# Low parts of the probabilities split in two halves, and tiny two-tensor operations issued as plain tensor products, in an attention and two-layer MLP kernel ordered by a planner

## The chip, the cores and the metric

The kernel runs on one core of one Trainium2 chip. The time is device microseconds (us) of one execution; the kernel before took 744.99 us in the median of three runs (744.27 to 745.95). The engines are called PE (matrix multiply), ACT (activations), DVE (vector), POOL (GpSimd) and SP (which issues the DMAs here).

## The reference

Attention with a hashed mask over 2 batches, 8 heads, 768 positions and a head size of 64, and then two MLPs over the 1536 tokens of width 512 with a hidden width of 2048:

```python
q_bits = (einsum('bhsd,dk->bhsk', q, proj) > 0); k_bits likewise     # 6 hash bits
mask   = q_bucket[..., :, None] == k_bucket[..., None, :]
scores = where(mask, q @ k.T / 8, -1e9);  scores -= max(scores)
attn   = exp(scores);  attn /= sum(attn) + 1e-9;  o = attn @ v
x = o as (tokens, 512)
x = silu(x @ moe_w_in) @ moe_w_out
x = hardswish(x @ moe2_w_in) @ moe2_w_out          # h * clip(h + 3, 0, 6) / 6
```

q, k, v and proj are float32, the weights float64. The kernel multiplies in float16 pairs: a value is split into a high part and a low part (what the high part lost), and a product is three matmuls: high by high, low by high, high by low.

## The kernel before, in words

**Attention.** A pair is two heads of one batch (8 pairs, 4 a batch). A unit is one pair and two of its six query tiles of 128 rows, so it has four slots (two tiles by two heads); there are 24 units and 96 slots. For each slot PE makes the 768 scores in PSUM (L819, L820); DVE takes their maximum (L823) and two tiny products of it (L825 `sc`, L828 `nb`); ACT takes the exponential and its sum (L831 into `e`, float32). The score buffers `s` are two, so the scores of a slot wait for the exponential of the slot two before it. Then there are two ways. In the first 32 slots (`exact_values`, two of three blocks of batch 0) PE turns `e` in float32 (L847), ACT copies the turned tile (L853; the planner may give a copy to DVE, L854) and PE multiplies by the values (L859). In the other 64 (`split_values`) ACT casts `e` to float16, the high part (L878; DVE instead is L879), POOL takes the low part `e - high` into the second half of the tile `PN` (L880), one transposing DMA turns both (L883), and PE multiplies (L873). At the end of a unit (`finish`) DVE makes reciprocals of the sums (L900, L903 and, for exact units, L905) and scales (L908), ACT and POOL split the result (L912, L913), a DMA turns it, and ACT squares it for a norm (L425).

**Weights and MLPs.** Each weight chunk of 512 KB arrives by DMA in a buffer `st` (three of them), with 64-bit words that ACT (L489), POOL (L490) and DVE (L492, L494) put together; then ACT (L431) and DVE (L437) split it into high and low. In `mlp1` a hidden tile is made by PE (L946), passes ACT's tanh (L989), a DVE product (L991) and a split (ACT L431, DVE L437 into `G`), and PE multiplies it by the second weight (L1003). `mlp2` does the same with a relu (L1078 to L1086) and L1091. The MLP of batch 0 runs beside the attention of batch 1.

**Small scales.** Norms and scales are columns of one tile `table`, 128x1 each. `mul` (L419) multiplies two of them and a constant in one `scalar_tensor_tensor` (L420).

**What sets the order.** `Plan` holds every operation with its engine (or two engines to choose from), a cost, and what it reads and writes. `Plan.issue` lays out the work 24 times with lists of ranks, judges each by ten randomised replays, and issues the best in that order; each engine then runs its own list in order. A cost table (`Cost`) has waits between engines, a slack behind DMAs, and a shared port: POOL operations, and DVE operations whose entry ends in `True`, are laid out so that they don't overlap. So any change of a cost, of a flag or of the number of operations gives another order on all engines.

Of the kernel before, what the change touches and what calls it, by code (L numbers as in the profile page):

```python
# [247 lines left out]
class Plan:  # L248
# [6 lines left out]
    def op(self, ways, reads=(), writes=(), take=None, give=None, before=(), turn=0):  # L255

        o = Op(ways if isinstance(ways, list) else [ways], take, give, turn, len(self.ops))
        for cell in writes:  # L260
            o.deps.update(self.writers.get(cell, ()))
            o.deps.update(self.readers.get(cell, ()))
        for cell in reads:
            assert cell in self.writers, cell
            o.deps.update(self.writers[cell])
        for cell in (*reads, *writes):
            if isinstance(cell, tuple) and isinstance(cell[0], Buf):
                b = cell[0]
                assert not b.closed, (b.tag, cell[1:])
                if b.prev is not None:  # L270
                    o.deps.update(b.prev.ops)
                b.ops.append(o)
        for cell in writes:
            self.writers[cell], self.readers[cell] = [o], []
        for cell in reads:
            if cell not in writes:
                self.readers.setdefault(cell, []).append(o)
        for d in o.deps:
            d.succ.append(o)
        for d in before:  # L280
            d.soft.append(o)
        self.ops.append(o)
        return o
# [26 lines left out]
def kernel(  # L310
# [63 lines left out]
    def buf(pool, tag, shape, dtype, bufs=1):  # L374
        return Buf(plan, pool, tag, shape, dtype, bufs)
# [12 lines left out]
    ident = const("ident", [P, P])  # L388
    op((POOL, 0.3, lambda: make_identity(nc, ident)), (), ["ident"])
    op((DVE, 0.1, lambda: nc.vector.memset(three, 3.0)), (), ["three"])  # L390
    ident16 = buf(ep, "PN", [P, P], F16, bufs=3)
    op((DVE, 0.14, lambda: nc.vector.tensor_copy(ident16.t, ident)), ["ident"], [(ident16, 0)])

# [20 lines left out]
    def pow2(o, hx, sign, base):  # L414
        nc.vector.tensor_scalar(
            o.bitcast(I32), hx, float(sign * 2**23), float(base * 2**23), op0=ALU.mult, op1=ALU.add
        )

    def mul(o, a, b, c=1.0):  # L419
        nc.vector.scalar_tensor_tensor(o, a, c, b, op0=ALU.mult, op1=ALU.mult)  # L420

    def square_sum(src, dst, n, reads, writes):
        def fn():
# [175 lines left out]
    xparts = const("xparts", [P, B, NU, HP])  # L599
    vparts = const("vparts", [P, B, HP])  # L600
    v_s = [const(f"v_s{b}", [P, 1]) for b in range(B)]
    v_i = [const(f"v_i{b}", [P, 1]) for b in range(B)]
    XT = [None] * B

    def heads(x, b, h0, n):
# [2 lines left out]
    def v_norm(b):  # L608
        ss = small().tile([P, 1], F32, tag=f"vss{b}", name="vss")
        op((DVE, 0.15, lambda: nc.vector.tensor_reduce(ss, vparts[:, b], op=ALU.add, axis=AX.X)),  # L610
           [("vp", b, i) for i in range(HP)], [("vss", b)])
        key, tot = total(lambda: ss, 1, [("vss", b)])

        def fn():
            hx = half_exp(tot, 1)
            pow2(v_s[b], hx, -1, 203)
            pow2(v_i[b], hx, 1, 51)

        op((DVE, 0.35, fn), [key], [("v_s", b)], give="m")

# [172 lines left out]
    class Unit:  # L793
# [71 lines left out]
        def split_values(self, e, po, a, cell):  # L865
            V = self.pair.V
            pn = buf(ep, "PN", [P, 2, S], F16, bufs=NPN)
            pt = buf(ep, "PT", [P, 2, T, P], F16, bufs=NPT)

            def values():  # L870
                for kt in range(T):
                    for i, (vh, pl) in enumerate(combos):
                        nc.tensor.matmul(  # L873
                            po(), pt.t[:, pl, kt, :], V.t[:, a, vh, kt * D : (kt + 1) * D],
                            start=(i == 0 and kt == 0), stop=(i == 2 and kt == T - 1),
                        )

            op(ways((ACT, Cost.act(S), lambda: nc.scalar.activation(pn.t[:, 0], e.t, AF.Copy)),  # L878
                    (DVE, 0.47, lambda: nc.vector.tensor_copy(pn.t[:, 0], e.t), True)), [(e, 0)], [(pn, 0)])  # L879
            op(ways((POOL, Cost.pool_tt(S), lambda: nc.gpsimd.tensor_tensor(pn.t[:, 1], e.t, pn.t[:, 0], op=ALU.subtract)),  # L880
                    (DVE, Cost.tt(S), lambda: nc.vector.tensor_tensor(pn.t[:, 1], e.t, pn.t[:, 0], op=ALU.subtract), True)),
               [(e, 0), (pn, 0)], [(pn, 1)])
            op((SP, Cost.turn(2 * T), lambda: nc.sync.dma_start_transpose(  # L883
                out=pt.t.rearrange("p h t c -> p (h t) c"), in_=pn.t.rearrange("p h c -> p (h c)"))),
               [(pn, 0), (pn, 1)], [(pt, 0)], turn=1)
            op((PE, 3 * T * Cost.mm(D), values), [(pt, 0), (V, 0), (V, 1)], [cell])

        def finish(self):
            pr, n, nt = self.pair, self.n, self.nt
            cells = [(qi, a) for qi in range(nt) for a in range(2)]  # L890
            rc = buf(small, "rc", [P, 2 * QT], F32, bufs=4)
            x = buf(ep, "x", [P, 2 * QT, D], F32, bufs=2)
            xn = buf(ep, "xn", [P, QT, 2, P], F16)
            if XT[pr.b] is None:
                XT[pr.b] = buf(tp, ("X0", "T3")[pr.b], [P, NK, T, 2, P], F16)
            xt = XT[pr.b]
            xq = lambda: x.t[:, :n].rearrange("p (q a) d -> p q (a d)", a=2)

            def reciprocals():
                nc.vector.tensor_scalar(  # L900
                    rc.t[:, :n], self.sm.t[:, :nt].rearrange("p q a -> p (q a)"), 1e-9 * PSC, None, op0=ALU.add
                )
                nc.vector.reciprocal(rc.t[:, :n], rc.t[:, :n])  # L903
                if self.exact:
                    nc.vector.tensor_scalar(rc.t[:, :n], rc.t[:, :n], v_s[pr.b], None, op0=ALU.mult)  # L905

            op((DVE, 0.5 if self.exact else 0.3, reciprocals, True), [(self.sm, *c) for c in cells] + [("v_s", pr.b)], [(rc, 0)])
# [46 lines left out]
    def mlp1(b, blk, pool):  # L954
# [15 lines left out]

        op((DVE, 0.34, start), [tk], [("mlp", key)], give="m")
        for g in range(W1I.n):
            op((DVE, 0.14, lambda g=g: mul(u1[:, g : g + 1], v_i[b], W1I.i[:, g : g + 1], 0.5), True),
               [("v_s", b), ("W1I", g)], [("u1", key, g)])
        G = buf(pool, "G", [P, NF, 2, n], F16)

# [44 lines left out]
        def finish():  # L1021
            hx = half_exp(tot2, 1)
            pow2(c2, hx, -1, 203)
            pow2(ci, hx, 1, 51)
            mul(ci, ci, cgi)
            mul(ci, ci, v_i[b], 0.5)
            mul(ci, ci, W1I.top)
            mul(ci, ci, W1O.i)

        op((DVE, 1.05, finish, True), [tk, ("mlp", key), ("W1O", 0), ("W1I", "top"), ("v_s", b)], [("c2", key)], give="m")  # L1030
        for j in tiles:
            c2i[b, j] = ci, ("c2", key)
        for m in range(NK):
# [162 lines left out]
```

## Time and profile before

| what | value |
|---|---|
| median of three runs | 744.99 us |
| the profiled execution, whole | 746.96 us |
| its span, first to last instruction | 745.2 us |
| PE, ACT, DVE, POOL busy | 693.0, 519.1, 507.5, 184.3 us |
| mean granted PE clock | 0.986 of full speed |

The profile is of one execution, 1.97 us above the median; 1.76 us of it lie outside the span. Busy time is the union of an engine's instructions. A PE instruction that waits shows as idle time before it, with the engine whose signal came last. The stages can be told apart by what runs: up to 128.6 us (the first L946) attention of batch 0 with the first weights arriving; to 204.5 us (the last split of the first MLP's weights) that MLP starts while its weights are still split; to 361.9 us (the last L913) batch 1's attention beside the MLP of batch 0; then MLPs alone.

### The profile page before, as it was taken

The numbers are of one execution on the slowest core, as the hardware profiler recorded it, in microseconds if no ns is written. First come the engines' busy times: TensorE is split into PE (matmuls) and PEld (weight loads), VectorE is DVE, ScalarE is ACT, GpSimd is POOL, SyncE is SP. The second block draws the span as 40 slices with busy tenths as digits, with TensorE's granted clock in tenths as the row PEclk, the third lists the DMA queues.
The fourth block names the chain that finished last, engine by engine and source line by source line (L and its number), as shares of the span: only waits on it lengthen the run. The fifth ranks groups of instructions, "written<-read, shape, count | busy, mean of one in ns | idle before, by whom it ended". The sixth has DMA issues, their size and how long they took to land.

```text
span 745.2 us, 15604 instructions
## 1 busy us (share of the span) xinstructions
PE 693.0 (93%) x6060; PEld 514.1 (69%) x6060; DVE 507.5 (68%) x1147; ACT 519.1 (70%) x1027; POOL 184.3 (25%) x182
## 2 busy tenths in 40 slices
PE   3799988776899999999999999999999999999997
PEld 3498877654688888888888888864445664444564
DVE  4898999999976886986695968883333443333443
ACT  7998999899988988898665858872334334233433
POOL 3111224544364656667222220000000000000000
PEclk9999999997999999999999999999999999999999
DMA  8798556999599889989845450000000000000100
GB/s 303 184 244 191 159 187 219 209 237 251 117 172 209 162 198 199 205 156 162 208 144 178 159 174 1 1 1 1 1 0 35 23 1 29 0 1 1 57 1 28
DMA packets 176265, 89.61 MB, mean 120 GB/s; under 512 B 158784, under 2 KB 165952, under 8 KB 176192
## 3 DMA queue, kind: packets, MB, share of 16 engines
q1 hardware_dynamic: 176192, 88.63, 49.4%
q8 instruction: 47, 0.77, 0.4%
q14 instruction: 26, 0.21, 0.1%
HBM read 44.57 MB, written 3.15 MB: 64 GB/s over the span
## 4 chain that ended last, share of the span: by engine, by line
PE 73%; DVE 11%; ACT 9%; issue 3%; DMA 2%; POOL 1%; SPq 0%; ACTq 0%; DVEq 0%; POOLq 0%
PE h L946 27%; PE s L1091 17%; PE h L1003 16%; PE o L859 3%; PE o L873 3%; PE s L819 3%; PE s L820 3%; DVE nm L823 2%; ACT sq L425 2%; ACT e L831 2%; PE h L847 1%; DVE w L494 1%; DVE table L420 1%; ACT w L431 1%; DMA w<-in_v_dram 1%
## 5 line engine op out<-in xcount | busy, mean ns | idle before, releaser
L1091 PE MATMUL s<-y,G 128*128 128x512 f16 x576 | 134.4, 379 | 0.8 <-ACT w L1107 0.8
L1003 PE MATMUL h<-G,w 128*128 128x256 f16 x1152 | 133.6, 273 | 0.1
L946 PEld LDWEIGHTS <-w 128*128 128x128 f16 x1152 | 113.1, 100 | 27.7 <-DVE g L991 10.3
L880 POOL TENSOR_TENSOR PN<-e,PN 128x768 f16<-128x768 f32 x64 | 110.0, 1722 | 78.0 <-ACT PN L878 49.5
L1003 PEld LDWEIGHTS <-w 128*128 128x128 f16 x1152 | 110.9, 98 | 15.0 <-DVE w L437 0.4
L1078 ACT ACTIVATE g<-h,table 128x256 f32<-128x256 f32 x96 | 50.7, 562 | 88.7 <-PE h L946 88.7
L823 DVE TENSOR_REDUCE nm<-s 128x1 f32<-128x768 f32 x96 | 91.2, 951 | 21.1 <-PE s L820 20.5
L831 ACT ACTIVATE e<-s,nb,sc 128x768 f32<-128x768 f32 x96 | 95.6, 996 | 10.5 <-DVE nb L828 8.7
L1091 PEld LDWEIGHTS <-G 128*128 128x128 f16 x576 | 56.3, 98 | 62.8 <-issue 1.1
L1082 DVE TENSOR_SCALAR g<-g 128x512 f32<-128x512 f32 (+1 forms) x64 | 23.1, 360 | 101.7 <-ACT g L1078 101.7
L946 PEld LDWEIGHTS <-T 128*128 128x128 f16 x576 | 56.4, 98 | 42.1
L946 PE MATMUL h<-X,w 128*128 128x256 f16 x576 | 75.8, 282 | 9.7 <-DVE g L991 9.7
L490 POOL TENSOR_SCALAR st<-st 128x512 f32<-128x512 f32 x64 | 47.8, 749 | 149.2 <-ACT w L489 65.3
L1085 ACT ACTIVATE G<-g 128x512 f16<-128x512 f32 (+1 forms) x64 | 33.4, 522 | 62.0 <-DVE g L1084 62.0
L819 PE MATMUL s<-T 128*128 128x384 f16 x192 | 65.0, 339 | 9.2 <-ACT e L831 9.1
L820 PE MATMUL s<-T 128*128 128x384 f16 x192 | 65.2, 340 | 0.0
L946 PE MATMUL h<-T,w 128*128 128x256 f16 x576 | 64.3, 272 | 0.4 <-DVE g L991 0.4
L1086 DVE TENSOR_TENSOR G<-g,G 128x512 f16<-128x512 f32 (+1 forms) x64 | 35.7, 559 | 40.4 <-ACT G L1085 40.4
L878 ACT ACTIVATE PN<-e 128x768 f16<-128x768 f32 x63 | 52.9, 841 | 2.7 <-DMA PT<-PN 2.6
L946 PE MATMUL h<-T,T 128*128 128x512 f16 (+1 forms) x288 | 50.7, 326 | 0.0
L946 PE MATMUL h<-X,T 128*128 128x512 f16 (+1 forms) x288 | 50.7, 326 | 0.0
L859 PE MATMUL o<-w,PT 128*128 128x64 f32 x384 | 46.8, 272 | 2.2 <-DVE sc L825 2.2
(128 smaller groups left out, 1117.4 us busy)
## 6 DMA issues: line engine op xcount, KB each, us to landing
st<-in_moe_w_in_dram SPq DMA_DIRECT2D x32, 512.0 KB, 4.6
st<-in_moe_w_out_dram SPq DMA_DIRECT2D x32, 512.0 KB, 3.9
qk<-in_v_dram SPq DMA_DIRECT2D x8, 384.0 KB, 3.5
out_dram<-w SPq DMA_DIRECT2D x12, 256.0 KB, 2.0
qk<-in_q_dram SPq DMA_DIRECT2D x6, 384.0 KB, 3.4
qk<-in_k_dram SPq DMA_DIRECT2D x6, 384.0 KB, 5.4
w<-in_v_dram SPq DMA_DIRECT2D x2, 768.0 KB, 8.8
T<-T SPq DMA_DIRECT2D x8, 192.0 KB, 2.8
```

Of the source, the lines that this page charges most:

```text
L490: op((POOL, Cost.pool_ts(512), lambda: nc.gpsimd.tensor_scalar(st.t[:, :, 1].bitcast(F32), st.t[:, :, 1].bitcast(F32), 0.0, 1.0, op0=ALU.m ...
L819: nc.tensor.matmul(o, t.t[:, 0, c, :], t.t[:, 1, ks, :], start=True, stop=False)
L820: nc.tensor.matmul(o, t.t[:, 2, c, :], t.t[:, 3, ks, :], start=False, stop=True)
L823: op((DVE, 0.865, lambda: nc.vector.tensor_reduce(nm.t, ps.t[:, :, :HS], op=ALU.max, axis=AX.XY, negate=True)), [(ps, 0)], [(nm, 0)])
L831: op((ACT, 0.97, lambda: nc.scalar.activation(e.t.rearrange("p (n c) -> p n c", n=2), ps.t[:, :, :HS], AF.Exp, bias=nb.t, scale=sc.t, accu ...
L859: nc.tensor.matmul(po(), pt.t[:, kt, :], vraw.t[:, v0 + a, kt * D : (kt + 1) * D], start=(kt == 0), stop=(kt == T - 1))
L878: op(ways((ACT, Cost.act(S), lambda: nc.scalar.activation(pn.t[:, 0], e.t, AF.Copy)), (DVE, 0.47, lambda: nc.vector.tensor_copy(pn.t[:, 0] ...
L880: op(ways((POOL, Cost.pool_tt(S), lambda: nc.gpsimd.tensor_tensor(pn.t[:, 1], e.t, pn.t[:, 0], op=ALU.subtract)), (DVE, Cost.tt(S), lambda ...
L946: nc.tensor.matmul(ph, W[f, wl, kt, :], XT[b].t[:, kt, ts, xl, :], start=(c == 0), stop=(c == 3 * NK - 1))
L1003: nc.tensor.matmul(pf.t[:, :n], W1O[f, wl, slice(m * P, (m + 1) * P)], G.t[:, f, gl], start=(f == 0 and c == 0), stop=(f == NF - 1 and c = ...
L1078: nc.scalar.activation(g.t[:, cs], pf.t[:, cs], AF.Relu, bias=three, scale=a)
L1091: nc.tensor.matmul(acc[m // 2].t[:, m % 2, :DM], gs.t[:, f % 3, gl, m * P : (m + 1) * P], W2O[f, wl], start=(f == 0 and c == 0), stop=(f = ...
```

## The change

A third column `least` holds the constant that is added to the sums. `mul` without a constant is a `tensor_tensor` of two 128x1 columns, and the scale of V's inverse, `v_i`, is kept halved (`v_h`), so that two of its uses need no constant. The addition of `least` and the product by `v_s` in the reciprocals become `tensor_tensor` with a broadcast column. Three entries lose the flag of the shared port (the reciprocals, `u1`, and the end of `mlp1`). The low part of a probability tile is two operations of 384 columns instead of one of 768, each free to go to POOL or to DVE; the transposing DMA waits for both.

```diff
     def mul(o, a, b, c=1.0):
-        nc.vector.scalar_tensor_tensor(o, a, c, b, op0=ALU.mult, op1=ALU.mult)
+        if c == 1.0:
+            nc.vector.tensor_tensor(o, a, b, op=ALU.mult)
+        else:
+            nc.vector.scalar_tensor_tensor(o, a, c, b, op0=ALU.mult, op1=ALU.mult)
...
-            pow2(v_i[b], hx, 1, 51)
+            pow2(v_h[b], hx, 1, 50)
...
-            op(ways((POOL, Cost.pool_tt(S), lambda: nc.gpsimd.tensor_tensor(pn.t[:, 1], e.t, pn.t[:, 0], op=ALU.subtract)),
-                    (DVE, Cost.tt(S), lambda: nc.vector.tensor_tensor(pn.t[:, 1], e.t, pn.t[:, 0], op=ALU.subtract), True)),
-               [(e, 0), (pn, 0)], [(pn, 1)])
+            for n in range(2):
+                c = slice(n * HS, (n + 1) * HS)
+                op(ways((POOL, Cost.pool_tt(HS), lambda c=c: nc.gpsimd.tensor_tensor(
+                            pn.t[:, 1, c], e.t[:, c], pn.t[:, 0, c], op=ALU.subtract)),
+                        (DVE, Cost.tt(HS), lambda c=c: nc.vector.tensor_tensor(
+                            pn.t[:, 1, c], e.t[:, c], pn.t[:, 0, c], op=ALU.subtract), True)),
+                   [(e, 0), (pn, 0)], [(pn, 1 + n)])
...
-                nc.vector.tensor_scalar(
-                    rc.t[:, :n], self.sm.t[:, :nt].rearrange("p q a -> p (q a)"), 1e-9 * PSC, None, op0=ALU.add
+                nc.vector.tensor_tensor(
+                    rc.t[:, :n], self.sm.t[:, :nt].rearrange("p q a -> p (q a)"), least.to_broadcast([P, n]), op=ALU.add
                 )
                 nc.vector.reciprocal(rc.t[:, :n], rc.t[:, :n])
                 if self.exact:
-                    nc.vector.tensor_scalar(rc.t[:, :n], rc.t[:, :n], v_s[pr.b], None, op0=ALU.mult)
-            op((DVE, 0.5 if self.exact else 0.3, reciprocals, True), ...
+                    nc.vector.tensor_tensor(rc.t[:, :n], rc.t[:, :n], v_s[pr.b].to_broadcast([P, n]), op=ALU.mult)
+            op((DVE, 0.5 if self.exact else 0.3, reciprocals), ...
...
-        op((DVE, 1.05, finish, True), [tk, ("mlp", key), ("W1O", 0), ("W1I", "top"), ("v_s", b)], [("c2", key)], give="m")
+        op((DVE, 1.05, finish), [tk, ("mlp", key), ("W1O", 0), ("W1I", "top"), ("v_s", b)], [("c2", key)], give="m")
```

The counts of what is issued stay almost the same. The new program issues 54 of the 60 products of `table` columns as `tensor_tensor`; all 64 low parts are on POOL in both, as 128 halves now; one copy L853 that was DVE's (L854) is ACT's, one cast L878 goes from ACT to DVE, one tiny `sc` from DVE to POOL, and one split of `mlp1` (L1035) from POOL to ACT. Line numbers of the new program are higher (L880 is L889, L831 is L837, L991 is L1002, L437 is L442, L492 and L494 are L497 and L499).

On POOL, in the attention of batch 1, the rows before (`PN` is the tile of both parts, `e` the exponentials, `xn` the result of a unit):

```order
L880 TENSOR_TENSOR PN_3470<-e_3365,PN_3470 128x768
L880 TENSOR_TENSOR PN_3499<-e_3443,PN_3499 128x768
L880 TENSOR_TENSOR PN_3572<-e_3533,PN_3572 128x768
L913 TENSOR_TENSOR xn<-x_3234,xn 128x2x128
L880 TENSOR_TENSOR PN_3648<-e_3581,PN_3648 128x768
```

and now:

```order
L889 TENSOR_TENSOR PN_3648<-e_3605,PN_3648 128x384 x2
L889 TENSOR_TENSOR PN_3695<-e_3657,PN_3695 128x384 x2
L889 TENSOR_TENSOR PN_3751<-e_3706,PN_3751 128x384 x2
L924 TENSOR_TENSOR xn<-x_3266,xn 128x2x128
L889 TENSOR_TENSOR PN_3837<-e_3797,PN_3837 128x384 x2
```

Both halves of a tile stand together on POOL; none has gone to DVE.

On ACT, the rows that end with the 48th exponential of the program, before (`w` are weights being split, `sq` are squares):

```order
L831 ACTIVATE e_2808,sm_2774<-s_2627,nb_2713,sc_2700 128x768
L431 ACTIVATE w_2803<-w_1847,table 128x512 x3
L431 ACTIVATE G<-g_2794,table 128x2x256
L878 ACTIVATE PN_2864<-e_2808 128x768
L912 ACTIVATE xn<-x_2255 128x2x128
L431 ACTIVATE w_2882<-w_2237,table 128x512 x2
L831 ACTIVATE e_2902,sm_2774<-s_2779,nb_2885,sc_2835 128x768
L431 ACTIVATE w_2882<-w_2237,table 128x512 x2
L878 ACTIVATE PN_2932<-e_2902 128x768
L831 ACTIVATE e_2941,sm_2774<-s_2830,nb_2906,sc_2904 128x768
```

and now:

```order
L837 ACTIVATE e_2875,sm_2852<-s_2740,nb_2799,sc_2785 128x768
L923 ACTIVATE xn<-x_2424 128x2x128
L436 ACTIVATE w_2781<-w_1931,table 128x512
L884 ACTIVATE PN_2912<-e_2875 128x768
L837 ACTIVATE e_2923,sm_2852<-s_2858,nb_2910,sc_2907 128x768
L430 ACTIVATE sq,xparts<-x_2424 128x256
L884 ACTIVATE PN_2960<-e_2923 128x768
L430 ACTIVATE sq,xparts<-x_2790 128x256
L837 ACTIVATE e_2980,sm_2852<-s_2917,nb_2975,sc_2965 128x768
```

The splits of weights stand earlier than before, but counted from the start of the program the same work is ahead of this exponential: 288 instructions before and 290 now (accumulator reads not counted), the two more being a copy L853 and a square L425 of a unit's result. PE's list ahead of the scores two slots later differs by six L1003 more, all other counts being equal.

On DVE, from the last weight chunks of the second MLP to the 42nd hidden tile of `mlp1` (L991, the last block of batch 1), before (`y` and `T` are weight tiles, `st` arriving chunks):

```order
L494 SCALAR_TENSOR_TENSOR y_7206<-st_7216,y_7206 128x512
L492 SCALAR_TENSOR_TENSOR y_7206<-y_7206,st_7246 128x512
L1017 TENSOR_REDUCE table<-table 128x1
L494 SCALAR_TENSOR_TENSOR y_7206<-st_7246,y_7206 128x512
L508 TENSOR_REDUCE table<-table 128x1
L991 SCALAR_TENSOR_TENSOR g_7358<-g_7358,h_7311 128x512
L409 TENSOR_SCALAR hx<-p_tot 128x1
L415 TENSOR_SCALAR table<-hx 128x1 x2
L437 SCALAR_TENSOR_TENSOR G<-g_7358,table,G 128x2x256
L991 SCALAR_TENSOR_TENSOR g_7389<-g_7389,h_7343 128x512
```

and now:

```order
L442 SCALAR_TENSOR_TENSOR T_7356<-T_6468,table,T_7356 128x512
L1028 TENSOR_REDUCE table<-table 128x1
L499 SCALAR_TENSOR_TENSOR y_7305<-st_7287,y_7305 128x512
L497 SCALAR_TENSOR_TENSOR y_7305<-y_7305,st_7328 128x512
L442 SCALAR_TENSOR_TENSOR T_7356<-T_6468,table,T_7356 128x512
L499 SCALAR_TENSOR_TENSOR y_7305<-st_7328,y_7305 128x512
L1002 SCALAR_TENSOR_TENSOR g_7451<-g_7451,h_7401 128x512
L497 SCALAR_TENSOR_TENSOR y_7305<-y_7305,st_7367 128x512
L442 SCALAR_TENSOR_TENSOR T_7460<-y_6618,table,T_7460 128x512
L499 SCALAR_TENSOR_TENSOR y_7305<-st_7367,y_7305 128x512
L1002 SCALAR_TENSOR_TENSOR g_7483<-g_7483,h_7436 128x512
```

Thirteen splits of the second MLP's weights that stood behind this tile stand ahead of it now, between the rows that put the last chunks together, and the last chunk comes behind the 41st hidden tile; PE's list has the same rows ahead of this tile's matmuls but for one tiny sum.

## Rows read from the trace of the kernel before

**Rows 1.** The page, busy us (share) and instructions of each engine

```profile
PE 693.0 (93%) x6060; PEld 514.1 (69%) x6060; DVE 507.5 (68%) x1147; ACT 519.1 (70%) x1027; POOL 184.3 (25%) x182
```

**Rows 2.** Busy us by stretch, granted clock, DMA share, GB/s

```profile
0.00:20.00 20.00, 6.99 (x66) 6.25 (x67) 9.93 (x35) 15.36 (x28) 6.78 (x23) 1.00 0.85 294
20.00:207.00 187.00, 155.11 (x1451) 130.49 (x1451) 176.50 (x419) 180.69 (x363) 59.11 (x59) 0.95 0.80 199
207.00:460.00 253.00, 250.32 (x2922) 218.09 (x2919) 194.58 (x433) 203.08 (x409) 118.40 (x100) 1.00 0.77 171
460.00:745.20 285.20, 280.58 (x1631) 159.27 (x1628) 126.54 (x264) 120.00 (x230) 0.00 (x0) 1.00 0.03 12
```

**Rows 3.** What PE waited for, 120 to 205 us: total, times, longest

```profile
PE h L946 <- DVE g L991: 9.7, 4, 4.4
PE s L819 <- ACT e L831: 5.4, 5, 2.3
```

**Rows 4.** What ACT waited for, 20 to 200 us

```profile
ACT N L431 <- DVE qksc L415: 1.5, 1, 1.5
ACT e L831 <- DVE nb L828: 1.4, 3, 0.8
ACT G L431 <- DVE g L991: 1.1, 1, 1.1
```

**Rows 5.** The chain that ended last, 124 to 160 us: start, us, what

```profile
129.26 1.49 DVE table L420
...
136.90 1.86 DVE w L494
...
141.24 1.49 DVE table L420
...
148.56 2.05 DVE G L437
...
156.82 2.05 DVE w L494
```

**Rows 6.** Instructions of single lines: duration ns min/median/max, first and last start

```profile
L420 DVE SCALAR_TENSOR_TENSOR table<-table x60: 146/159/1490, 66.2 to 498.0; 128x1 f32<-128x1 f32 x60
L420 DVE SCALAR_TENSOR_TENSOR table<-inv x8: 159/160/1600, 7.6 to 252.8; 128x1 f32<-128x1 f32 x8
...
L437 DVE SCALAR_TENSOR_TENSOR G<-g,table,G x48: 721/746/2130, 148.5 to 473.3; 128x512 f16<-128x512 f32 x48
...
L494 DVE SCALAR_TENSOR_TENSOR w<-st,w x32: 675/682/2129, 17.3 to 175.6; 128x512 int32<-128x512 int32 x32
...
L900 DVE TENSOR_SCALAR rc<-sm x24: 154/160/635, 39.6 to 350.6; 128x4 f32<-128x4 f32 x24
...
L908 DVE TENSOR_TENSOR x<-o,rc x24: 406/415/426, 44.5 to 360.9; 128x256 f32<-128x256 f32 x24
```

**Rows 7.** Instructions on the tiles PN and xn, POOL's

```profile
L880 POOL TENSOR_TENSOR PN<-e,PN x64: 1639/1647/2376, 126.8 to 351.7; 128x768 f16<-128x768 f32 x64
...
L913 POOL TENSOR_TENSOR xn<-x,xn x24: 666/673/1403, 53.0 to 361.9; 128x256 f16<-128x256 f32 x24
```

**Rows 8.** Groups of instructions: busy us, mean ns, idle before

```profile
L1003 PE MATMUL h<-G,w 128*128 128x256 f16 x1152 | 133.6, 273 | 0.1
...
L853 ACT ACTIVATE PT<-h 128x384 f32<-128x384 f32 x63 | 28.7, 505 | 0.8 <-PE h L847 0.6
...
L425 ACT ACTIVATE sq<-x 128x256 bf16<-128x256 f32 x24 | 10.1, 422 | 0.9 <-DVE x L908 0.9
...
L437 DVE SCALAR_TENSOR_TENSOR T<-T,table,T 128x512 f16<-128x512 f32 x8 | 5.7, 744 | 0.0
...
L425 ACT ACTIVATION_READ_ACCUMULATOR sq<-x 128x1 f32 x24 | 5.0, 207 | 0.0
```

**Rows 9.** Busy us from 436 us to the 41st hidden tile on DVE

```profile
436.00:452.30 16.30, 16.30 (x152) 14.61 (x151) 9.43 (x14) 9.83 (x22) 4.55 (x6) 1.00 0.40 131
```

More of the change, by code (lines that the diff above doesn't have):

```diff
@@ L390 @@
     op((DVE, 0.1, lambda: nc.vector.memset(three, 3.0)), (), ["three"])
+    least = const("least", [P, 1])
+    op((DVE, 0.1, lambda: nc.vector.memset(least, 1e-9 * PSC)), (), ["least"])
     ident16 = buf(ep, "PN", [P, P], F16, bufs=3)
@@ L601 @@
     v_s = [const(f"v_s{b}", [P, 1]) for b in range(B)]
-    v_i = [const(f"v_i{b}", [P, 1]) for b in range(B)]
+    v_h = [const(f"v_h{b}", [P, 1]) for b in range(B)]
     XT = [None] * B
@@ L879, in split_values @@
                     (DVE, 0.47, lambda: nc.vector.tensor_copy(pn.t[:, 0], e.t), True)), [(e, 0)], [(pn, 0)])
-            op(ways((POOL, Cost.pool_tt(S), lambda: nc.gpsimd.tensor_tensor(pn.t[:, 1], e.t, pn.t[:, 0], op=ALU.subtract)),
-                    (DVE, Cost.tt(S), lambda: nc.vector.tensor_tensor(pn.t[:, 1], e.t, pn.t[:, 0], op=ALU.subtract), True)),
-               [(e, 0), (pn, 0)], [(pn, 1)])
+            for n in range(2):
[5 more added lines that the diff above has]
+                   [(e, 0), (pn, 0)], [(pn, 1 + n)])
             op((SP, Cost.turn(2 * T), lambda: nc.sync.dma_start_transpose(
                 out=pt.t.rearrange("p h t c -> p (h t) c"), in_=pn.t.rearrange("p h c -> p (h c)"))),
-               [(pn, 0), (pn, 1)], [(pt, 0)], turn=1)
+               [(pn, 0), (pn, 1), (pn, 2)], [(pt, 0)], turn=1)
             op((PE, 3 * T * Cost.mm(D), values), [(pt, 0), (V, 0), (V, 1)], [cell])
@@ L904, in reciprocals @@
                 if self.exact:
-                    nc.vector.tensor_scalar(rc.t[:, :n], rc.t[:, :n], v_s[pr.b], None, op0=ALU.mult)
-            op((DVE, 0.5 if self.exact else 0.3, reciprocals, True), [(self.sm, *c) for c in cells] + [("v_s", pr.b)], [(rc, 0)])
+                    nc.vector.tensor_tensor(rc.t[:, :n], rc.t[:, :n], v_s[pr.b].to_broadcast([P, n]), op=ALU.mult)
+            op((DVE, 0.5 if self.exact else 0.3, reciprocals), ["least", ("v_s", pr.b)] + [(self.sm, *c) for c in cells], [(rc, 0)])
             op((DVE, Cost.tt(n * D), lambda: nc.vector.tensor_tensor(
@@ L972, in mlp1 @@
         for g in range(W1I.n):
-            op((DVE, 0.14, lambda g=g: mul(u1[:, g : g + 1], v_i[b], W1I.i[:, g : g + 1], 0.5), True),
+            op((DVE, 0.14, lambda g=g: mul(u1[:, g : g + 1], v_h[b], W1I.i[:, g : g + 1])),
                [("v_s", b), ("W1I", g)], [("u1", key, g)])
@@ L1025, in finish @@
             mul(ci, ci, cgi)
-            mul(ci, ci, v_i[b], 0.5)
+            mul(ci, ci, v_h[b])
             mul(ci, ci, W1I.top)
             mul(ci, ci, W1O.i)
-        op((DVE, 1.05, finish, True), [tk, ("mlp", key), ("W1O", 0), ("W1I", "top"), ("v_s", b)], [("c2", key)], give="m")
+        op((DVE, 1.05, finish), [tk, ("mlp", key), ("W1O", 0), ("W1I", "top"), ("v_s", b)], [("c2", key)], give="m")
         for j in tiles:
```

## The prediction

> **What bounds the kernel now.** I read the page's busy times first. PE is busy for 693.0 of 745.2 us [rows 1], so all a better order can win is PE's 52.2 us of idle time. The table of busy time by stretch shows where they lie [rows 2]: 13.0 us in the first 20, 31.9 between 20 and 207, 2.7 between 207 and 460, 4.6 after that, mostly at the end. PE's list is the same work in any order, so the question is the stretch from 20 to 207. There ACT is busy for 180.69 of 187 us and DVE for 176.50: both are nearly full, ACT more so, and PE waits for both. The list of PE's waits says how [rows 3]: 9.7 us in four waits for DVE's product in the first MLP, which frees the PSUM buffer of a hidden tile, and 5.4 us in five waits for ACT's exponential. After 207 us PE's idle time is too small to win much from.
>
> So the time of this kernel is: PE's rows, plus how far ACT's and DVE's rows run ahead of PE's by the time that PE has enough to do. ACT's 6.31 us of idle time in the stretch are the most that ACT's own finish can come forward without taking work off it. Of these, the waits put down to DVE are 1.5 + 1.4 + 1.1 = 4.0 us [rows 4].
>
> DVE is late partly through waits inside its instructions. The chain that ended last is DVE's from 124 to 160 us, and five of its pieces there are longer than the same instructions elsewhere [rows 5]: the products L420 at 129.26 and 141.24 (1.49 us each, median 0.16), L494 at 136.90 and 156.82 (1.86 and 2.05, median 0.68) and L437 at 148.56 (2.05, median 0.75) [rows 5, 6]. The excess is 1.33 + 1.18 + 1.33 + 1.30 + 1.37 = 6.5 us. No excess is longer than one low-part operation on POOL (1.647 us), and all five come after the first of those, at 126.8 us [rows 7]: DVE stands still while POOL works on a tile.
>
> **The change part by part.** The new order. The planner lays out everything anew, so I counted what stands ahead of one and the same point. Ahead of the 48th exponential ACT has 288 instructions before and 290 now. The two more are a copy L853, 28.7 / 63 = 0.46 us, and a square with its accumulator read, (10.1 + 5.0) / 24 = 0.63 us [rows 8]. PE has six L1003 more ahead of the scores that wait for that exponential, 6 x 133.6 / 1152 = 0.70 us [rows 8], which it does earlier. Net: +1.09 - 0.70 = +0.4 us. On ACT the weight splits come sooner and the exponentials later in between, but what is due by then is the same.
>
> The low parts in halves. From 256 columns (0.673 us) to 768 (1.647) a column costs 1.9 ns [rows 7], so a half of 384 is an estimated 0.917 us and a pair 1.83: 0.19 us more for each of 64 tiles, 12.0 us on POOL. POOL is busy for 59 of 187 and 118 of 253 us in the two stretches [rows 2], so its throughput hides it; but the transposing DMA and the products behind it start 0.19 us later for each tile. If each delay reached PE that would be 12.0 us. It can't win time here, since both halves wait for the whole cast and stand together on POOL. I take 0: between 207 and 460 us, where some 48 of the 64 tiles pass, PE idles for 2.7 us in all, and a passage that is a tenth longer scales that by 0.3 us.
>
> What the halves do win is DVE's waits: a DVE instruction that meets POOL waits for 0.917 us at most instead of 1.647, 0.56 of it. If each half lets DVE in between, four of the five waits above, 5.18 us (all but the L420 at 141.24, which changes its form; the one at 129.26 has a constant and keeps its form), shrink by 2.3 us. The other end is that POOL goes through with both halves and nothing is won.
>
> The tiny products. 54 of 60 become plain products of two columns. A wait like that at 141.24, 1.33 us, goes if the new form doesn't meet POOL, and stays if it does. No row before shows a tiny product of two SBUF tensors beside POOL. The nearest rows differ: L908, a plain product with one operand in PSUM, never exceeds 0.426 us, while the L420 and L437 with two operands in SBUF reach 1.490 and 2.130 [rows 6]. By its form the new operation is like L908, by where its operands lie like L437. I let it go in the sum, and keep the other as a rival. The reciprocals' addition, now with a second operand, reached 0.635 once, with 0.160 the median [rows 6]: whichever way it goes is under half a microsecond.
>
> The Trainium skill's page "SBUF — State Buffer", section "Who interferes with whom", speaks against the tiny products: a DVE instruction with two SBUF inputs contends with a GpSimd instruction that reads SBUF, and the second to issue waits for the whole first. The trace agrees for L437 and L908; for a 128x1 product no run here shows it. By this rule the wait at 141.24 would only shrink to 0.56, and the saving of all five be 0.44 x 6.51 = 2.9 us instead of 3.6.
>
> The sum. The two parts take 2.3 + 1.33 = 3.6 of 6.5 us of DVE's waits on the chain, 55%. But DVE's gain counts only as far as ACT is not the limit: 4.0 us of ACT's idle time are DVE's, and 55% of them are 2.2 us. The bounds of this term are 0 and 4.0. So 745.2 + 0.4 - 2.2 = 743.4 us of span; with the 1.76 us around it, 745.2 us for the profiled execution, which stands 1.97 above the median of the runs: **743.2 us**.
>
> What I cost at nothing. The four operations that change engine: the L879 cast and the copy given up are under 0.6 us each on DVE. The late weights: by the 42nd hidden tile of the MLPs DVE has 13 more weight splits ahead, 13 x 5.7 / 8 = 9.3 us [rows 8], PE nothing; the cover is DVE's idle time, 16.30 - 9.43 = 6.9 us between 436 and 452 us [rows 9], and what it has earlier. If the splits can't use these gaps, up to 9.3 us reach PE. The DMA queue issues the same transfers in a new order; I price that through the rows that wait for them, as above.
>
> **The rivals.** *Nothing comes off.* POOL goes through with both halves and the tiny products wait as before, with two SBUF operands each; the planner, which no longer keeps three kinds of them clear of POOL, sends more of them into it. Then only the count remains: 745.0 + 0.4 = 745.4 us. For it speaks that L437 has two such operands and waits; against it that half an operation is a shorter hold.
>
> *The second MLP's weights get in the way (slower).* The last chunk's DVE row now stands behind the 41st hidden tile and ahead of the 42nd, so a hidden tile waits for a transfer and three engines' work on it. PE makes the hidden tiles of the last block in one run there, with two buffers, and has nothing else in its list between. Against it: PE was never idle between 436 and 452 us [rows 9]. It decides when the gaps take less of the 9.3 us than that: with the 6.9 us all used, 2.4 us come out; with none, 9.3. On top of my forecast that is 745.6 to 752.5 us; I take 749.
>
> *More than I say.* ACT's whole idle time goes, 6.3 us, since earlier weight splits give PE products to fill its four waits for DVE. For it: the splits stand earlier on ACT. Against: the same rows are due by the 48th exponential. 745.0 + 0.4 - 6.3 = 739.1 us.
>
> By the skill's rule alone the saving is 44% of 4.0 instead of 55%, so 743.6 us; it lies within my case's range.
>
> **How the numbers follow.** My case, 743.2 us, has a chance of 0.43 and its own range, by the bounds 0 and 4.0 of its term, is 741.4 to 745.4. Nothing comes off: 0.22. Weights in the way: 0.20. More: 0.15. About 0.2% is what a measurement here can tell from no change, so faster is below 743.5 and slower above 746.5. Faster: 0.27 of my case, all 0.15 of the last and 0.01 of the second, 0.43. Same: 0.16, 0.13 of nothing and 0.02 of the late weights, 0.31. Slower: 0.18 of the late weights and 0.08 where nothing comes off and the longer POOL passes reach PE, 0.26. The range goes from 738.5, below the third rival, to 749.5, the middle of the second: outside are about 0.1 above and 0.05 below.
>
> **What would show it.** Right: PE's idle time between 20 and 207 us at 30 us or a little less, ACT still over 95% busy there; L437 and L494 with maxima near 1.6 us (0.75 and 0.68 plus 0.92) instead of 2.1; the tiny products at 0.17 us with no maximum over 0.3; the POOL half at 0.9 us. A maximum of 1.1 us in the tiny products would show the rule on two SBUF inputs right. Wrong: PE idle for 2 us or more between 436 and 480 us, waiting for the product of a hidden tile; or PE's idle time between 207 and 360 us grown, with waits for the transposing DMA. The point that would make the whole argument wrong is an ACT that is well below 95% busy before 207 us, since then the count ahead of the 48th exponential isn't what holds PE.

## The result: slower, 751.2 us where 743.2 was forecast

| kernel | median | lowest to highest | ratio to before (95%) |
|---|---|---|---|
| before | 744.81 us (4 runs) | 744.27 to 745.95 | |
| after | 751.23 us (4 runs) | 749.84 to 753.36 | 1.0087 [1.0060, 1.0113] |

The prediction had the sign wrong; the time lies above its range too. The profiled execution of after took 749.84 us (span 748.1), 1.4 below its median, while that of before lay 2.15 above: the two profiles show 2.9 of the 6.4 us between the medians, and I lean on single profiles only where several kernels agree. Beside the experiments below, the runs of before spread from 743.6 to 755.8 us (granted clock 0.993 to 0.972), so a ratio there can differ from the quotient of the two medians by up to 0.3%; one run of E1, of 1457 us, is left out of its ratio.

The table of busy time by stretch, of after, answers [rows 2]:

```profile
0.00:20.00 20.00, 6.81 (x67) 6.19 (x68) 10.04 (x37) 15.76 (x29) 7.17 (x23) 1.00 0.84 285
20.00:207.00 187.00, 153.51 (x1426) 129.09 (x1426) 176.31 (x423) 177.73 (x357) 60.20 (x73) 0.95 0.83 198
207.00:460.00 253.00, 251.22 (x2911) 216.94 (x2910) 198.20 (x431) 208.99 (x423) 131.41 (x150) 0.99 0.80 172
436.00:480.00 44.00, 44.00 (x407) 39.47 (x405) 40.61 (x81) 35.99 (x70) 5.61 (x6) 1.00 0.23 71
```

Between 20 and 207 us ACT idles for 9.27 us instead of 6.31, and PE for 33.5 instead of 31.9. After 207 us PE is as full as before. Around the 42nd hidden tile (436 to 480) it is never idle: the second MLP's weights are not in its way.

What PE (120 to 205 us) and ACT (20 to 207) waited for, of after, against [rows 3, 4] (up to 207 us, before has the same three rows of [rows 4]):

```profile
PE h L957 <- DVE g L1002: 6.9, 4, 3.0
PE s L825 <- ACT e L837: 4.8, 4, 2.5
...
ACT G L436 <- DVE g L1002: 3.5, 2, 2.1
ACT e L837 <- DVE nb L834: 2.5, 3, 2.1
ACT w L494 <- DMA st<-in_moe_w_in_dram: 1.6, 3, 1.3
ACT PT L859 <- PE h L853: 1.4, 4, 0.8
```

ACT's waits for DVE were meant to shrink from 4.0 us; they are 6.0, with one of 1.6 for a DMA beside them. The longest for `nb` comes last: the 47th exponential starts at 205.0 us after 2.1 us of idle time, and PE's next scores wait 2.8 us for it. DVE had two rows of two columns to do ahead of this exponential's maximum, `hx` and `qksc`, which took 0.91 and 0.84 us beside POOL halves (0.17 is the median of either).

Single lines of after, against [rows 6, 7] (duration ns min/median/max):

```profile
L889 POOL TENSOR_TENSOR PN<-e,PN x128: 903/913/1804, 134.5 to 356.6; 128x384 f16<-128x384 f32 x128
...
L423 DVE TENSOR_TENSOR table<-table x54: 129/159/842, 69.4 to 505.3; 128x1 f32<-128x1 f32 x54
...
L442 DVE SCALAR_TENSOR_TENSOR G<-g,table,G x48: 736/746/1415, 138.8 to 476.1; 128x512 f16<-128x512 f32 x48
L442 DVE SCALAR_TENSOR_TENSOR w<-w,table,w x32: 735/745/1481, 91.5 to 204.8; 128x512 f16<-128x512 f32 x32
...
L499 DVE SCALAR_TENSOR_TENSOR w<-st,w x32: 677/684/1165, 18.7 to 160.3; 128x512 int32<-128x512 int32 x32
...
L417 DVE TENSOR_SCALAR table<-hx x42: 143/150/156, 22.7 to 499.9; 128x1 int32<-128x1 int32 x42
L417 DVE TENSOR_SCALAR qksc<-hx x8: 169/170/841, 7.1 to 245.1; 128x2 int32<-128x2 int32 x8
```

A POOL half takes 0.913 us, and DVE's longest waits are shorter by about what was forecast: `G` reaches 1.42 us instead of 2.13. The tiny product still waits, up to 0.84 us. The chain that ended last, of after, still runs through DVE there, with shorter pieces than in [rows 5] but more kinds of them:

```profile
138.82 1.19 DVE G L442
140.01 1.33 DVE w L497
...
145.14 0.84 DVE qksc L417
...
150.83 1.42 DVE N L442
```

So the halves did what they should, the tiny products did not, and the time was lost elsewhere. Where, the 48th exponential shows. Its row in ACT's timeline, of before, of after, and of the kernel E1 below (the old order with the new forms):

```profile
204.64 1.01 ACT L831 ACTIVATE e<-s,nb,sc 128x768 f32<-128x768 f32 x1
```

```profile
207.53 0.98 ACT L837 ACTIVATE e<-s,nb,sc 128x768 f32<-128x768 f32 x1
```

```profile
201.18 0.98 ACT L840 ACTIVATE e<-s,nb,sc 128x768 f32<-128x768 f32 x1
```

And the table of busy time up to that start, in the same sequence:

```profile
0.00:204.60 204.60, 159.70 (x1487) 134.92 (x1488) 184.06 (x448) 193.64 (x384) 64.01 (x81) 0.95 0.80 209
```

```profile
0.00:207.50 207.50, 160.82 (x1497) 135.71 (x1498) 186.81 (x460) 193.99 (x387) 67.51 (x97) 0.96 0.83 207
```

```profile
0.00:201.20 201.20, 158.50 (x1485) 133.50 (x1486) 178.05 (x448) 193.22 (x385) 64.37 (x95) 0.97 0.82 213
```

From there to the end of the span it is 745.2 - 204.6 = 540.6, 748.1 - 207.5 = 540.6 and 741.5 - 201.2 = 540.3 us: between these three kernels the start of this exponential decides. ACT's work ahead of it is equal to 0.8 us; its idle time, the stretch minus ACT's busy time, is 10.96, 13.51 and 7.98 us.

### The profile page after: what moved, and what is told of

It reads as the page before. It is cut to its first block, busy times and chain, and to the rows that moved or that the text cites. A ratio compares the mean times of both kernels' runs of the same rounds, so it can differ in the third digit from the quotient of the medians.

```text
span 748.1 us, 15741 instructions
## 1 busy us (share of the span) xinstructions
PE 695.2 (93%) x6060; PEld 514.3 (69%) x6060; DVE 506.0 (68%) x1147; ACT 518.3 (69%) x1028; POOL 198.8 (27%) x246
## 4 chain that ended last, share of the span: by engine, by line
PE 64%; DVE 16%; ACT 9%; DMA 6%; issue 4%; SPq 0%; POOL 0%; ACTq 0%; DVEq 0%
PE h L957 26%; PE s L1102 17%; PE h L1014 13%; DVE nm L829 4%; ACT e L837 2%; DMA PT<-PN 2%; PE o L865 2%; DMA st<-in_moe_w_in_dram 2%; PE s L825 2%; PE s L826 2%; DVE w L442 2%; PE o L879 2%; DVE G L442 1%; ACT sq L430 1%; DMA T<-N 1%
## 5 line engine op out<-in xcount | busy, mean ns | idle before, releaser
L889 POOL TENSOR_TENSOR PN<-e,PN 128x384 f16<-128x384 f32 x128 | 123.0, 983 | 70.4 <-issue 31.8
L1014 PE MATMUL h<-G,w 128*128 128x256 f16 x1152 | 135.7, 274 | 1.8 <-DVE g L1002 1.7
L837 ACT ACTIVATE e<-s,nb,sc 128x768 f32<-128x768 f32 x96 | 95.2, 994 | 11.4 <-DVE nb L834 5.5
L495 POOL TENSOR_SCALAR st<-st 128x512 f32<-128x512 f32 x64 | 49.9, 781 | 146.8 <-ACT w L494 63.9
L957 PE MATMUL h<-X,w 128*128 128x256 f16 x576 | 73.0, 278 | 6.9 <-DVE g L1002 6.9
```

The source lines that it names most:

```text
L495: op((POOL, Cost.pool_ts(512), lambda: nc.gpsimd.tensor_scalar(st.t[:, :, 1].bitcast(F32), st.t[:, :, 1].bitcast(F32), 0.0, 1.0, op0=ALU.m ...
L837: op((ACT, 0.97, lambda: nc.scalar.activation(e.t.rearrange("p (n c) -> p n c", n=2), ps.t[:, :, :HS], AF.Exp, bias=nb.t, scale=sc.t, accu ...
L889: op(ways((POOL, Cost.pool_tt(HS), lambda c=c: nc.gpsimd.tensor_tensor(pn.t[:, 1, c], e.t[:, c], pn.t[:, 0, c], op=ALU.subtract)), (DVE, C ...
L957: nc.tensor.matmul(ph, W[f, wl, kt, :], XT[b].t[:, kt, ts, xl, :], start=(c == 0), stop=(c == 3 * NK - 1))
L1014: nc.tensor.matmul(pf.t[:, :n], W1O[f, wl, slice(m * P, (m + 1) * P)], G.t[:, f, gl], start=(f == 0 and c == 0), stop=(f == NF - 1 and c = ...
```

## The experiments

Every ratio is to the kernel before, run beside it, with its 95% interval. Letters and theories in the quotes hold for their own group.

**Forms and order apart: E1 to E4.** The halves are emitted inside one planner entry of the old cost, and the tiny products without touching flags, so the layout stays that of before (`...` stands for code that is left out):

```diff
+            def low_halves():
+                for n in range(2):
+                    c = slice(n * HS, (n + 1) * HS)
+                    nc.gpsimd.tensor_tensor(pn.t[:, 1, c], e.t[:, c], pn.t[:, 0, c], op=ALU.subtract)
-            op(ways((POOL, Cost.pool_tt(S), lambda: ...pn.t[:, 1], e.t, pn.t[:, 0]...
+            op(ways((POOL, Cost.pool_tt(S), low_halves),
```

E3 has this alone, E4 the tiny products alone (the other hunks of the change, flags kept), E1 both. E2 is the reverse, after's order with the old forms:

```diff
-                            pn.t[:, 1, c], e.t[:, c], pn.t[:, 0, c], op=ALU.subtract)),
+                def low_whole(n=n):
+                    if n == 1:
+                        nc.gpsimd.tensor_tensor(pn.t[:, 1], e.t, pn.t[:, 0], op=ALU.subtract)
```

E1: 

> Every engine's list as in the kernel before; only the forms are new: each low part as two halves on POOL, 54 products of two columns and the reciprocals as tensor_tensor. Theory 1, the new order costs the time and the forms don't: ratio 0.997 to 1.003 to the kernel before (743 to 747 us). Theory 2, the forms cost it (more and shorter meetings of DVE and POOL, 12 us more on POOL): ratio 1.006 or more, 749.5 to 752 us.

E2: 

> Every engine's list as in the changed kernel; only the forms are old: one low part of 768 columns in the place of the two halves, scalar_tensor_tensor and tensor_scalar for the tiny operations. Theory 1, the order costs the time: ratio 1.006 to 1.011, 749 to 753 us. Theory 2, the forms cost it: 0.997 to 1.003, 743 to 747 us.

E3: 

> The order before, and of the forms the halves alone. If halves shorten DVE's waits without cost: DVE's maxima in L437 and L494 near 1.4 to 1.6 us instead of 2.1 and 742 to 745 us. If only the longer POOL passes count: 745 to 747 us, with POOL's low part at 0.9 us a half.

E4: 

> The order before, and of the forms the tiny two-tensor operations alone. If a tensor_tensor of two columns doesn't meet POOL: no tiny product over 0.3 us, 743 to 744.5 us. If it meets POOL like the old form: products up to 1.5 us remain (low parts are whole here), additions of the reciprocals over 0.6 us appear, and 744.5 to 746 us.

| | old order | new order |
|---|---|---|
| old forms | 1 | E2 1.0096 [1.0060, 1.0131] |
| tiny products alone | E4 0.9977 [0.9940, 1.0013] | |
| halves alone | E3 **0.9937** [0.9902, 0.9972] | |
| both | E1 0.9951 [0.9920, 0.9982] | after 1.0087 [1.0060, 1.0113] |

The order costs 1.0% with the old forms and 1.4% with the new; the forms win 0.5% in the old order, by E3 through the halves. E3, 743.67 us beside 746.48 of before in the median (0.4%, where the ratio has 0.6%), beats both kernels. Its waits in DVE and those of E4 show which part did it; single lines of E3, then of E4:

```profile
L437 DVE SCALAR_TENSOR_TENSOR G<-g,table,G x48: 721/745/1403, 144.3 to 468.0; 128x512 f16<-128x512 f32 x48
...
L420 DVE SCALAR_TENSOR_TENSOR table<-table x60: 130/158/833, 64.3 to 492.7; 128x1 f32<-128x1 f32 x60
```

```profile
L427 DVE TENSOR_TENSOR table<-table x54: 145/158/1645, 66.4 to 497.0; 128x1 f32<-128x1 f32 x54
...
L446 DVE SCALAR_TENSOR_TENSOR G<-g,table,G x48: 720/745/2129, 148.4 to 472.4; 128x512 f16<-128x512 f32 x48
```

With the halves an old-form tiny product waits to 0.83 us; with whole tiles a new-form one waits to 1.65, like an old one. The halves shorten the waits, the new form doesn't remove them. ACT's idle time ahead of the 48th exponential in E3 is 199.90 - 193.34 = 6.6 us, against 10.96 of before:

```profile
0.00:199.90 199.90, 158.79 (x1486) 133.97 (x1487) 179.01 (x447) 193.34 (x385) 64.57 (x95) 0.97 0.82 214
```

**Where in the order: E5, E6, E9, E10.** New forms; every engine's list follows one order up to an exponential and the other behind it (how the stored order is unpacked is left out):

```diff
-        for i in best.order:
-            next(w[2] for w in self.ops[i].ways if w[0] == best.engines[i])()
+        for i, e in ORDER:          # one order up to the cut, the rest as in the other
+            next(w[2] for w in self.ops[i].ways if w[0] == e)()
```

E5: 

> New forms; the old order up to the 48th exponential (about 205 us), from there the new order. If the new order loses its time before 205 us (PE's waits for exponentials and hidden tiles, half clock after them): 742 to 745 us, like the old order with new forms. If it loses it in the late part, for instance where the second MLP's weight splits stand ahead of the last hidden tiles: 748 to 751 us.

E6: 

> New forms; the new order up to the 48th exponential, from there the old order: the other half of the same question. If the loss lies before 205 us: 749 to 752 us, with PE idle for 3 us more than with the old order between 120 and 207 us. If it lies later: 742 to 745 us.

E9: 

> New forms everywhere; every engine's list is the old order up to the 34th exponential (about 126 us, just ahead of the first hidden tile), then the new order's. Theory A, that the new order loses its time between 126 and 205 us, where ACT idled for 6.4 us against 1.0 in the old order: ratio to the kernel before 1.006 to 1.010, as the whole change, and ACT idle for over 4 us between 120 and 207. Rival, that it is lost earlier (the first weights, the exact units) and the waits after 126 us are its consequence: 0.997 to 1.001, as with the cut at the 48th exponential (0.9986). 1.002 to 1.005: both.

E10: 

> The mirror image: new forms, the new order up to the 34th exponential, then the old order. Theory A: 0.994 to 0.998, as the old order with the new forms (0.9951), ACT idle for under 2 us between 120 and 207. Rival (lost before 126 us): 1.004 to 1.008, as with the cut at the 48th exponential (1.0061).

Cut at the 48th: old then new 0.9986 [0.9952, 1.0020], new then old 1.0061 [1.0021, 1.0101]. Most of the loss is ahead of it. Cut at the 34th: 1.0093 [1.0059, 1.0127], as theory A has it, and 1.0111 [1.0090, 1.0132], above both theories; no theory allows the pair. My reading, which no run tests: what one order does early the other does late, so a splice in the middle of the weights' work makes a third order, and it doesn't localise. E5 also gives the scatter: its lists up to the 48th exponential are E1's, yet that starts at 204.8 us in its profile and at 201.2 in E1's.

The new order's profiles agree on where ACT waits for DVE ahead of this exponential. Of E6 (20 to 220 us), whose lists up to there are after's, of E2 (20 to 207), the same lists with the old forms, and of E1 (20 to 207):

```profile
ACT G L438 <- DVE g L1003: 3.5, 2, 2.1
ACT e L838 <- DVE nb L835: 2.5, 3, 2.1
```

```profile
ACT e L834 <- DVE nb L831: 4.4, 3, 3.9
ACT G L433 <- DVE g L1002: 3.5, 2, 2.1
```

```profile
ACT e L840 <- DVE nb L837: 1.6, 4, 0.8
ACT w L440 <- DVE w L446: 0.3, 1, 0.3
```

In after, E6 and E2 it is the same three waits: two splits of a hidden tile wait for DVE's product of it (1.3 us near 155 us and 2.1 near 177), and the 47th exponential waits for its `nb` (2.1 us, 3.9 with the old forms). In after they come to 5.5 us. In the old order (before, E1, E3, E4, E5) no wait for such a product is longer than 1.1 us, and none of an exponential than 0.93.

**Whether the layout is a draw: E7, E8, E11, E12, O1 to O4.** The planner's inputs or its choice among its 24 layouts are changed:

```diff
 # E7 (after, layout 19), E8 (before, layout 5); O1, O2 (E11, E12 with layouts 13 and 19)
+            if n == 19:
+                best = run
 # E11: E1 with the three flags off; E12: after with the three flags kept
 # O3: E12 without the first True, O4: E12 without the second and third
-            op((DVE, 0.5 if self.exact else 0.3, reciprocals, True), ...
+            op((DVE, 0.5 if self.exact else 0.3, reciprocals), ...
-            op((DVE, 0.14, lambda g=g: mul(u1[:, g : g + 1], v_h[b], W1I.i[:, g : g + 1]), True),
+            op((DVE, 0.14, lambda g=g: mul(u1[:, g : g + 1], v_h[b], W1I.i[:, g : g + 1])),
-        op((DVE, 1.05, finish, True), ...
+        op((DVE, 1.05, finish), ...
```

E7: 

> The changed kernel with another of the planner's 24 layouts (the one with index 19 in place of 14; all else as in the changed kernel). If the new inputs (halves as two operations, no port flag on three kinds) make worse layouts as such: 749 to 753 us again. If one layout among 24 is a draw with its own real time: anything from 741 to 753 us, and not the same as the changed kernel's.

E8: 

> The kernel before, unchanged but for the layout: the planner's layout with index 5 in place of 18. If layouts are a draw: more than 0.4% away from the kernel before in one way or the other (up to 753 us). If the planner's old inputs give good layouts: within 0.3% of it, 743 to 747 us.

E11: 

> All emitted instructions in the new forms, laid out anew from the planner's inputs of before with one difference: the three entries (reciprocals, u1, end of mlp1) have lost the flag of the shared port; a pair of halves is one entry again. Theory A, that the old inputs happened to give a good layout and any new input draws another: the two cells of this pair fall without a pattern between 0.995 and 1.010. Theory B, that without the flags the planner lays out worse: 1.006 to 1.010 here, and under 1.000 in the run with the flags kept.

E12: 

> The changed kernel with the three flags of the shared port put back, laid out anew: the only inputs of the planner that differ from before are the halves as two entries, the dependence on the column least and the order of dependences. Theory C, that two entries per tile make the planner's layout worse: 1.006 to 1.010 here, and under 1.000 in the run without the flags. Theory A (a draw): no pattern between the two, and 0.995 to 1.010.

O1: 

> Same inputs of the planner as the run with the flags off and one entry per tile (1.0101), but layout 13 of its 24 is issued instead of layout 16. Theory B, without the three flags the layouts are worse: 1.005 to 1.011. Theory A, each layout is a draw between 0.995 and 1.011 whatever the flags: any value there; 1.000 or less would speak for A.

O2: 

> Same inputs as the run with the flags kept and the halves as two entries (0.9996), but layout 19 instead of 15. Theory B: 0.995 to 1.002. Theory A: any value between 0.995 and 1.011; 1.006 or more would speak for A.

O3: 

> The changed kernel with the flags of u1 and of the end of mlp1 put back, that of the reciprocals (24 entries) left off, laid out anew. Theory B with the reciprocals as the cause, since they stand in the attention stretch where the time is lost: 1.006 to 1.011 here and 0.995 to 1.002 in the run that keeps their flag. Theory A: no such pattern.

O4: 

> The changed kernel with only the flag of the reciprocals put back, those of u1 and of the end of mlp1 left off, laid out anew. Theory B with the reciprocals as the cause: 0.995 to 1.002. Theory B with the other two as the cause: 1.006 to 1.011, and 0.995 to 1.002 in the run without the reciprocals' flag. Theory A: no pattern.

Worked out from each profile by the table of busy time up to the 48th exponential:

| kernel | flags of `u1` and the end | 48th starts, us | ACT busy, idle ahead | DVE rows ahead | ratio (95%) |
|---|---|---|---|---|---|
| before | on | 204.6 | 193.6, 11.0 | 448 | 1 |
| E8 | on | 202.0 | 192.3, 9.8 | 437 | 1.0020 [0.9988, 1.0051] |
| E12 | on | 202.0 | 192.6, 9.4 | 449 | 0.9996 [0.9966, 1.0025] |
| O2 | on | 202.8 | 192.3, 10.5 | 446 | 1.0018 [0.9994, 1.0042] |
| O3 | on | 202.8 | 190.1, 12.7 | 442 | 0.9986 [0.9968, 1.0004] |
| after | off | 207.5 | 194.0, 13.5 | 460 | 1.0087 [1.0060, 1.0113] |
| E7 | off | 216.6 | 197.8, 18.8 | 469 | 1.0093 [1.0055, 1.0130] |
| E11 | off | 206.3 | 192.6, 13.7 | 461 | 1.0101 [1.0076, 1.0126] |
| O1 | off | 209.8 | 194.8, 15.1 | 465 | 1.0094 [1.0073, 1.0114] |
| O4 | off | 210.9 | 194.3, 16.7 | 460 | 1.0115 [1.0101, 1.0130] |

Not a draw. All five layouts without these flags are at 1.0087 to 1.0115, the five with them at 0.9986 to 1.0020 (by medians 1.009 to 1.011, and 0.999 to 1.005). The three flags came under suspicion with E11 and E12; O1 to O4 were built afterwards to test it, and all four fall on the side that their flags of `u1` and the end say. My first guess among the three, the reciprocals, was wrong (O3, O4). The halves as two entries and the reciprocals' flag do no harm (E12, O3). To the planner O4 differs from E12 in the two flags alone. On average the 48th exponential starts at 210.2 instead of 202.8 us, 7.4 later, of which 4.9 are ACT's idle time and 2.5 work put ahead of it; the ratios differ by 0.0094, 7.0 us. That holds on average only: from this exponential to the end of the span the ten take 535.9 us (E7) to 546.8 (E8). Of the 4.9 us, 2.8 are waits for DVE (3.6 us on average with the flags, 2.7 to 4.7; 6.3 without, 4.3 to 7.7) and 1.5 waits for PE; those for DMAs are equal (4.5 and 4.6). The granted clock up to there doesn't part them: 0.92 to 0.96 with the flags, 0.91 to 0.96 without. The rows of O3 and of O4 up to it:

```profile
0.00:202.80 202.80, 161.41 (x1469) 135.20 (x1470) 181.46 (x442) 190.06 (x380) 64.36 (x96) 0.92 0.83 210
```

```profile
0.00:210.90 210.90, 165.37 (x1502) 136.89 (x1503) 189.37 (x460) 194.25 (x387) 74.11 (x97) 0.95 0.78 202
```

**Whether it is the early `u1` products: O5, O6.** DVE has 460 to 469 rows ahead of the 48th exponential in the layouts without the flags and 437 to 449 in the others. The rows that tell all of them apart are products of two columns of `table`, 24 against 7 to 13: `u1` of hidden tiles that come much later. They stand like this in the timeline of DVE in after, and in E1 behind the exponential:

```profile
149.58 0.41 DVE L423 TENSOR_TENSOR table<-table 128x1 f32<-128x1 f32 x5
...
154.48 0.50 DVE L423 TENSOR_TENSOR table<-table 128x1 f32<-128x1 f32 x6
```

```profile
207.96 1.37 DVE L427 TENSOR_TENSOR table<-table 128x1 f32<-128x1 f32 x11
```

```diff
 # ORDER of O5 (after's order; in O6 E1's order and the reverse move)
-  11 x op u1 (second batch), ahead of the 48th exponential
+  11 x op u1 (second batch), right behind it
```

O5: 

> The changed kernel's order on every engine, but the 11 products u1 that stand on DVE between 122 and 155 us, for hidden tiles that come after 260 us, stand behind the 48th exponential, as the old order has them. Theory U, the 11 products themselves delay the exponentials: 0.995 to 1.001. Rival L, they cost their own 11 x 0.15 = 1.7 us of DVE at most and the rest of the order is the cause: 1.006 to 1.009.

O6: 

> The mirror image: the old order with the new forms (0.9951), but the 11 products stand as early as their operands allow, eight of them in one burst ahead of the two products of an exponential around 125 us. Theory U: 1.003 to 1.010. Rival L: 0.995 to 0.998.

O5 1.0076 [1.0047, 1.0105]: no gain worth the name (after has 1.0087), so these products are not what makes the new order slow. O6, 1.0003 [0.9966, 1.0040], is between the two theories: 0.5% above E1, with intervals that overlap, so standing early may cost something in the old order or nothing. Their rows up to the 48th exponential, O5 and O6:

```profile
0.00:209.80 209.80, 162.06 (x1492) 136.15 (x1493) 185.81 (x448) 194.09 (x388) 67.95 (x97) 0.96 0.80 205
```

```profile
0.00:206.30 206.30, 163.27 (x1485) 137.12 (x1486) 184.22 (x459) 193.51 (x384) 68.07 (x95) 0.95 0.80 207
```

O5 has DVE's 448 rows again and ACT still idles for 15.7 us; its profile has the three waits of after again (1.1, 3.4 and 2.1 us). What else the missing flags move on DVE, so that these rows come late, and which of the two matters, stays open. In the other layouts without the flags ACT waits for other rows of DVE (in E11 3.4 us for one weight split, in O4 6.6 us for `nb` in ten waits).

## Why the prediction was wrong, by its own steps

**The failed step is the new order at +0.4 us, "what is due by then is the same".** The count was right for what it counted: ACT is busy for 193.99 instead of 193.64 us ahead of the 48th exponential, +0.35. But a count of work says nothing of waits, and the start of a row is work plus waits. With the new forms in both, ACT idles for 7.98 us ahead of it in the old order and 13.51 in the new: +5.5 us where the step had 0, and three waits for DVE come to that much. Of this size one profile can't be sure: the same lists idle for 10.9 us in E5 and 14.6 in E6, so the pairs differ by 2.6 to 6.7 us. By time the order costs (1.0087 - 0.9951) x 745 = 10 us, in E2 7 us. I also counted ACT and PE only. DVE had 12 rows more ahead of that point (460 for 448); it would have been a sign that the order had changed in substance, though O5 shows that 11 of these rows are not the cause. The missing flags stand in the rival "Nothing comes off", but there only for more meetings with POOL; what they do to the rest of the layout was not priced.

**The frame held for one layout's variants.** From the 48th exponential to the end the profiles of before, after and E1 to E6 take 539.9 to 543.0 us, and ACT's idle time is most of what is won or lost ahead of it. For other layouts it is only a mean: the ten above spread by 11 us there.

**DVE's waits, -2.2 us (0 to -4.0): right in kind.** With the order held, E1's ratio is 0.5% under before (3.7 us) and its median 1.8 us; E3's ratio is 0.6% under. By E3 and E4 the halves gave it. ACT's waits for DVE, forecast at 4.0 - 2.2 = 1.8 us, are 1.9 in E1 and 2.0 in E3 ahead of the 48th exponential, but 3.7 in E5 with E1's lists, so the size is not settled. The term let the tiny products go free (1.33 of its 3.6 us), and that part was wrong: E4's product with two SBUF operands waited for a whole POOL operation (1.645 us). Rows 6 had said so for one column: L420 reads two columns of `table` too and reached 1.490 us. The Trainium skill's page "SBUF — State Buffer", section "Who interferes with whom", that a DVE instruction with two SBUF inputs contends with a GpSimd instruction that reads SBUF, held here at one column, with 1.645 us against a median of 0.158.

**POOL's 12 us at nothing: right.** The half took 0.913 us (estimate 0.917), and E3 is faster with it.

**The late weights at nothing: right.** DVE took the splits in its gaps, and PE was busy for 44.00 of 44.00 us. So the rival that was to end on the slow side had the wrong place; none of the three put a loss ahead of 207 us.

**The signs named.** ACT above 95% busy was too weak a line: after's 177.73 of 187 us is 95.0%, just on its right side, while before has 96.6% and E1 98.0%. PE's 33.5 us of idle time (30 or less was the sign of being right) and the tiny products' 0.84 us (0.3 at most) told it plainly; the maxima of `G` and of L499 (1.42 and 1.17 us), the POOL half and PE's full 44 us came out as the prediction said.

## What to carry to other kernels

When an order is laid out anew, don't price it by counting work ahead of a point: its waits change too, and here they moved the time by 1%, twice what the edit itself won. Two flags on tiny operations can do that (five layouts without them against five with), so try an edit with the order held before giving the planner new inputs. Splitting a long POOL operation shortens what a DVE instruction waits for (`G`'s longest fell from 2.13 to 1.40 us in E3); the two-tensor form didn't get round that wait (1.645 us in E4).

## What the runs showed of the hardware

A tensor-by-scalar row of two columns, `qksc` (128x2), waited up to 0.841 us beside a POOL half in after (three of eight rows, all beside a half), while the same line on one column kept to 0.156 at most over 42 rows, four of which stood beside a half too (both forms are among the single lines of after above).

PE's busy time hides its clock. In the second layout without the flags (O1) PE is about half idle from 120 to 130 us, and in the next 10 us its granted clock is 0.50, so 1.2 GHz; 38 matmuls then fill 8.06 us, where 118 fill 10.00 a little later. The mix of shapes differs, but one shape tells the same: a score matmul of 384 columns takes 527 ns at 128.1 us, where the granted clock is already 0.50, and 326 ns in the median of nine from 145 to 160 us. Busy time by stretch, of O1:

```profile
110.00:120.00 10.00, 9.13 (x75) 7.78 (x72) 9.93 (x24) 10.00 (x23) 2.73 (x4) 1.00 0.77 243
120.00:130.00 10.00, 4.29 (x27) 3.14 (x26) 9.86 (x26) 9.94 (x22) 4.54 (x6) 0.86 0.54 156
130.00:140.00 10.00, 8.06 (x38) 6.24 (x38) 7.50 (x23) 8.17 (x14) 6.76 (x7) 0.50 0.65 175
140.00:150.00 10.00, 10.00 (x118) 8.48 (x118) 7.95 (x20) 6.76 (x13) 1.86 (x2) 0.78 0.79 180
```
